# Two PSUM tiles instead of one for a step's first products, in a pool that takes over the projections' banks

## The chip, the cores and the metric

The kernel runs on one core of one Trainium2 chip. The metric is the device time of one execution in microseconds (us), lower is better. TensorE is called PE in the profile (PEld is its weight load), VectorE DVE, ScalarE ACT, GpSimd POOL, and SyncE, which only issues DMAs here, SP.

## The reference

Linear attention by exponential features, and a feed-forward layer with a Mish on what it gives:

```python
def phi(x):                                     # x: batch 8, heads 8, seq 576, head_dim 64
    proj = x @ w_phi                            # 64 -> 128
    proj = proj - np.max(np.abs(proj), axis=-1, keepdims=True)
    return np.concatenate([np.exp(proj), np.exp(-proj)], axis=-1)
q_p, k_p = phi(q), phi(k)
kv = einsum('bhsf,bhsd->bhfd', k_p, v); z = k_p.sum(axis=2)
attn = (q_p @ kv) / (q_p . z + 1e-6)
x = attn as (4608 tokens, 512)
h = x @ w_in                                    # 512 -> 2048
g = h * tanh(log1p(exp(h)))                     # Mish; h above 20 as it is
return g @ w_out                                # 2048 -> 512
```

## The kernel before, in words

All is float32. The program has one list of events, each with a planned time, sorted by that time; what stands in the sorted list is the order of every engine's queue. No engine changes its order at run time, so each stands still until the instruction at its head has what it waits for.

The first stage, to about 292 us, is the attention; its projections (`project`) go to PSUM tiles of two banks, tag `pp` of the pool `ps_a`, which has two of them and so holds four of the eight banks. The pool `ps_b` holds the other four, one bank for each of its tiles. The results go to DRAM (`x_spill`).

The second stage is the feed-forward layer. Tokens come in nine blocks of 512 (`sc`), the 2048 hidden units in eight blocks of 256 (`fp`). A step `n` is one `sc` with one `fp`; there are 72. The steps of one `sc` that follow each other without a break are a segment: four segments of two steps (steps 0 to 7), then sixteen of four. For each segment the activations are loaded (`x_load`), combined (`x_sum`) and split into a high and a low part (`x_block`: ACT casts the high one, DVE subtracts for the low one, seven blocks `xc`). A float32 product is made of three matmuls on such parts.

`h` of a step, 2 x 2 blocks of 128 x 256, comes out of a Winograd form of the 2 x 2 block product, with seven products instead of eight. With `h` as two banks of two halves, the step runs so:

- `ff_in(n, 0)`, PE: products 0 and 1 go to the two halves of the first bank, products 2 and 3 to the two halves of the second; six matmuls each, 24 in all.
- `first_product`, ACT: copies product 0 out as `p1`. `winograd` 0, 1, 2, DVE: `u2` = product 1 + `p1`; `u4` = product 2 + `u2`; the fourth block of `u` = product 3 + `u4`.
- `ff_in(n, 1)`, PE: product 4 is added onto product 0 in the first bank, products 5 and 6 onto 2 and 3 in the second bank; 18 matmuls.
- `mish(n, 0)`, ACT, reads the first bank's half 0; `winograd` 3, DVE, reads the whole second bank and adds `u2`; `mish(n, 1)`, `g_hi` (ACT) and `g_lo` (DVE) make the Mish and its two parts `gh` and `gl`.
- `ff_out`, PE: 24 matmuls of 128 x 512 on `gh`, `gl` and `wout`, in two halves. Products of older steps lie between the two parts of `ff_in`.

In the order written for steady steps PE runs 24 matmuls of `ff_in(n+1, 0)`, 12 of `ff_out`, 18 of `ff_in(n+1, 1)`, 12 of `ff_out`; ACT runs `p1` of step n+1 ahead of `mish(n, 1)` and `g_hi(n)`.

Between DMAs and the 16 pieces of weights that are still to be converted at that time (`weight_ops` with `quiet`: DVE and POOL, lines L124 to L186, in the second stage to about 603 us) the DVE queue also holds `x_sum` (L365), the low parts of `x_block` (L374) and the additions of `drain` (L462).

Waits are put in by the recording layer, by tile: two accesses to one PSUM tile by different engines are ordered by the last access to that tile, whichever of its banks it was. `h` of a step is one tile, `[P, 2, 2, CH]`, that uses the tag `pp` of `ps_a` after the projections:

```python
h_live[n] = ps_a.tile([P, 2, 2, CH], F32, tag="pp", name=f"h_{n}")
```

Of the kernel before, what the change touches and what calls it, by code (L numbers as in the profile page):

```python
# [8 lines left out]
F32 = mybir.dt.float32  # L9
F32R = mybir.dt.float32r  # L10
U32 = mybir.dt.uint32
AF = mybir.ActivationFunctionType
ALU = mybir.AluOpType
AX = mybir.AxisListType
PSUM = bass.MemoryType.PSUM

P = 128
# [5 lines left out]
CH = 256  # L23
# [34 lines left out]
def attention_then_mish(ctx, tc, qT, kT, va, w_phi, w_in, w_out, out):  # L58
    nc = tc.nc

    const = ctx.enter_context(tc.tile_pool(name="const", bufs=1))
    ffn = ctx.enter_context(tc.tile_pool(name="ffn", bufs=2))
    ps_a = ctx.enter_context(tc.tile_pool(name="ps_a", bufs=2, space=PSUM))
    ps_b = ctx.enter_context(tc.tile_pool(name="ps_b", bufs=4, space=PSUM))
    att_scope = ExitStack()
    att = att_scope.enter_context(tc.tile_pool(name="att", bufs=2))
    late = None
# [279 lines left out]
    xT, xc, h_live, u_live, g_live, o_live, part_live = {}, {}, {}, {}, {}, {}, {}  # L347
# [29 lines left out]
    def ff_in(n, which):  # L377
        s, sc, fp, first, last = steps[n]
        assert not any(("in", fp, k) in pieces_left for k in range(2))
        if which == 0:  # L380
            h_live[n] = ps_a.tile([P, 2, 2, CH], F32, tag="pp", name=f"h_{n}")
        for i in range(4) if which == 0 else range(4, 7):
            wb, xb, bank, half = PRODUCTS[i]
            ps = h_live[n][:, bank, half]
            m = 0
            for k in range(2):
                wh, wl = win[fp][:, k, 0, wb], win[fp][:, k, 1, wb]
                xh, xl = xc[s][xb][:, 0, k], xc[s][xb][:, 1, k]
                for w, x in ((wh, xh), (wh, xl), (wl, xh)):
                    nc.tensor.matmul(ps, w, x, start=(i in (0, 2) and m == 0), stop=(m == 5), skip_group_check=True)  # L390
                    m += 1

    def first_product(n):
        p1 = ffn.tile([P, CH], F32, tag="p1", name=f"p1_{n}", bufs=2)
        nc.scalar.copy(p1, h_live[n][:, 0, 0])  # L395
        u_live[n] = [p1]

    def winograd(n, i):
        ps = h_live[n]
        if i == 0:  # L400
            u2 = ffn.tile([P, CH], F32, tag="u2", name=f"u2_{n}", bufs=2)
            nc.vector.tensor_tensor(u2, ps[:, 0, 1], u_live[n][0], op=ALU.add)  # L402
            u_live[n].append(u2)
        if i == 1:
            u4 = ffn.tile([P, CH], F32, tag="u4", name=f"u4_{n}", bufs=1)
            nc.vector.tensor_tensor(u4, ps[:, 1, 0], u_live[n][1], op=ALU.add)
            u_live[n].append(u4)
        if i == 2:
            u = ffn.tile([P, 4, CH], F32, tag="u", name=f"u_{n}", bufs=2)
            nc.vector.tensor_tensor(u[:, 3], ps[:, 1, 1], u_live[n][2], op=ALU.add)  # L410
            u_live[n].append(u)
        if i == 3:
            u2, u = u_live[n][1], u_live[n][3]
            nc.vector.tensor_tensor(u[:, 1:3], ps[:, 1], u2.unsqueeze(1).broadcast_to([P, 2, CH]), op=ALU.add)  # L414

    def mish(n, which):
        u = u_live[n][3]
        if which == 0:
            nc.scalar.activation(u[:, 0], h_live[n][:, 0, 0], AF.Mish)  # L419
        else:  # L420
            nc.scalar.activation(u[:, 1:4], u[:, 1:4], AF.Mish)  # L421
            del h_live[n]
# [58 lines left out]
    def at(time, fn, *args):  # L481
        events.append((time, len(events), fn, args))

    def base(step):
        if step < 0:
            return step * LEAD_STEP
        return min(step, NU - LEAD) * STEP + max(0, step - NU + LEAD) * TAIL_STEP
# [33 lines left out]
    begin = base(NU + 2) + JOIN  # L521
# [5 lines left out]

    at(begin - 0.5, close)

    def t_of(n):  # L530
        return begin + 5.6 + (n - AHEAD) * FFSTEP if n >= AHEAD else begin - PRE[0] + PRE[1] * n

# [16 lines left out]
    for s, (sc, fps) in enumerate(segs):  # L549
        n = steps.index((s, sc, fps[0], True, fps[0] == fps[-1]))  # L550
        t = t_of(n - 2) if n >= AHEAD + 2 else begin - (X0_AT[0], 20)[s]
        at(t + 1.0, x_load, s, sc)
        for i in range(4):
            at(t + 5.5 + 0.7 * i, x_sum, s, i)
        t = t_of(n - 1) if n >= AHEAD + 2 else begin - (X0_AT[1], 3.9)[s]
        for b in range(7):
            at(t + (4.9 if n >= AHEAD + 2 else 3.5) + 0.8 * b, x_block, s, b)
    for n, (s, sc, fp, first, last) in enumerate(steps):
        t = t_of(n)
        at(t, ff_in, n, 0)  # L560
        at(t + 0.75, first_product, n)
        for i in range(3):
            at(t + 1.5 + 0.7 * i, winograd, n, i)
        second = t + 5.7 if n >= AHEAD else t + 3.0
        at(second, ff_in, n, 1)
        at(second + 2.3, winograd, n, 3)
        after = t_of(n + 1) if n >= AHEAD else begin - 2.0 + 2 * n
        at(second + 0.8 if n >= AHEAD else begin - 2.0 + 2 * n, mish, n, 0)
        at(after + 0.9, mish, n, 1)
        at(after + 1.8, g_hi, n)  # L570
        at(after + (3.7 if n >= AHEAD else 2.8), g_lo, n)
        out_a = (begin + 0.9, t_of(n + 1) + 2.8, t_of(n + 1) + 7.8)[min(n, 2)]
        out_b = t_of(n + 2) + 2.85 if n else begin + 2.7
        at(out_a, ff_out, n, 0)
        at(out_b, ff_out, n, 1)
        if last:
            at(t - 4.0 if n >= AHEAD else begin, part_load, s, sc)
            for tt in range(4):
                at((out_a, out_b)[tt // 2] + 1.4 * (tt % 2 + 1) + 0.1, drain, n, tt)
# [3 lines left out]
    for fp in range(HALF, NFP):  # L583
        n = max(i for i, st in enumerate(steps) if st[2] == fp - HALF)
# [41 lines left out]
```

## Time and profile before

| | |
|---|---|
| median of 3 runs | 1071.36 us (1069.99 to 1073.84) |
| the profiled execution's own time | 1071.71 us |
| its span, first to last instruction | 1069.9 us |
| mean granted clock of PE | 0.996 |
| busy: PE, PEld, DVE, ACT, POOL | 98%, 89%, 63%, 47%, 24% of the span |
| first product of the feed-forward layer starts at | 293.2 us |

The profiled execution lies 0.35 us above the median. In rows of the timeline the columns are the start in us, the duration in us of the merged row, engine, line, operation, tiles and count; in brackets stands how long the engine had been idle and whose instruction ended that.

### The profile page before, as it was taken

What the parts mean: (1) busy time and instruction counts of PE and PEld (TensorE: products, weight loads), DVE (VectorE), ACT (ScalarE), POOL (GpSimd) and SP (SyncE); (2) the same over time, 40 slices, a digit from 0 to 9 for tenths busy, and PEclk for the clock granted to TensorE, in tenths of its full rate; (3) what the DMA queues carried; (4) which work ended last, traced back from release to release, by engine and by line L of the source; (5) the groups of instructions that cost most, each with busy time, mean ns of one, the idle gap of its engine ahead of it and who ended that gap; (6) DMA issues with size and microseconds to landing.
All of it is one profiled execution on the core that took longest, in us unless ns stands there. A gap on an engine that the chain in (4) does not pass through costs nothing.

```text
span 1069.9 us, 25646 instructions
## 1 busy us (share of the span) xinstructions
PE 1049.1 (98%) x11200; PEld 951.5 (89%) x11200; DVE 672.7 (63%) x1005; ACT 497.5 (47%) x870; POOL 251.5 (24%) x213
## 2 busy tenths in 40 slices
PE   7999999999989999999999999999999999999998
PEld 7899999998979889998989899999999999999997
DVE  5888888877646877576575653554554546554543
ACT  4777777767744444344443433432332424324321
POOL 0544425532610454345462300000000000000000
PEclk9999999999999999999999999999999999999999
DMA  5545646666437525414424217543032131230221
GB/s 190 184 148 168 207 139 244 223 203 204 169 125 290 192 94 187 158 60 153 168 75 158 74 45 265 207 158 116 14 109 75 44 119 39 81 119 20 99 79 40
DMA packets 62943, 145.53 MB, mean 136 GB/s; under 512 B 5104, under 2 KB 25712, under 8 KB 60016
## 3 DMA queue, kind: packets, MB, share of 16 engines
q1 hardware_dynamic: 62832, 143.90, 38.7%
q8 instruction: 88, 1.44, 0.5%
q14 instruction: 23, 0.19, 0.1%
HBM read 96.17 MB, written 47.71 MB: 134 GB/s over the span
## 4 chain that ended last, share of the span: by engine, by line
PE 92%; DVE 4%; ACT 1%; DMA 1%; issue 1%; POOL 1%; SPq 0%; DVEq 0%; POOLq 0%
PE o L454 34%; PE h L390 32%; PE kvps L225 7%; PE num L225 7%; PE dt L293 4%; PE pp_q L210 4%; PE pp_k L210 4%; DVE xc L374 2%; PE xt L336 2%; DMA x<-x_spill 1%; DVE gl L431 0%; DVE u L414 0%; POOL w_in L168 0%; DMA kraw<-kT 0%; ACT xc L373 0%
## 5 line engine op out<-in xcount | busy, mean ns | idle before, releaser
L390 PEld LDWEIGHTS h<-xc,win 128*128 128x128 f32 x3024 | 381.7, 192 | 19.8 <-issue 5.5
L390 PE MATMUL h<-xc,win 128*128 128x256 f32 x3024 | 387.2, 283 | 6.6 <-DVE u L410 5.4
L454 PE MATMUL o<-wout,gh 128*128 128x512 f32 x1152 | 358.5, 392 | 0.0
L454 PEld LDWEIGHTS o<-wout,gh 128*128 128x128 f32 x1152 | 207.6, 189 | 36.0
L454 PE MATMUL o<-wout,gl 128*128 128x512 f32 x576 | 224.3, 389 | 2.1 <-DVE gl L431 2.1
L402 DVE TENSOR_TENSOR u<-h,p 128x256 f32<-128x256 f32 x72 | 30.5, 424 | 213.6 <-ACT p L395 213.6
L395 ACT COPY p<-h 128x256 f32<-128x256 f32 x72 | 26.8, 372 | 294.0 <-PE h L390 294.0
L454 PEld LDWEIGHTS o<-wout,gl 128*128 128x128 f32 x576 | 108.2, 188 | 26.7 <-DVE gl L431 3.2
L431 DVE TENSOR_TENSOR gl<-u,gh 128x1024 fp32r<-128x1024 f32 x72 | 92.3, 1283 | 31.9 <-ACT gh L426 31.9
L419 ACT ACTIVATE u<-h 128x256 f32<-128x256 f32 x72 | 27.7, 384 | 148.0 <-PE h L390 143.1
L299 ACT ACTIVATE e_q<-dt 128x512 f32<-128x512 f32 x144 | 77.2, 598 | 19.8 <-PE dt L293 19.6
L225 PE MATMUL kvps<-v,e_k 128*64 128x65 f32 x2560 | 83.0, 224 | 2.2 <-issue 1.2
L225 PEld LDWEIGHTS kvps<-v,e_k 128*64 128x64 f32 x2560 | 79.5, 140 | 3.0 <-issue 1.3
L414 DVE TENSOR_TENSOR u<-h,u 128x512 f32<-128x512 f32 x72 | 49.5, 687 | 48.8 <-ACT u L419 47.7
L426 ACT CAST gh<-u 128x1024 fp32r<-128x1024 f32 x72 | 75.8, 1053 | 2.2
L225 PE MATMUL num<-kv,e_q 128*64 128x65 f32 x2304 | 75.0, 223 | 0.0
L225 PEld LDWEIGHTS num<-kv,e_q 128*64 128x64 f32 x2304 | 70.1, 137 | 4.4 <-issue 0.3
L374 DVE TENSOR_TENSOR xc<-x,xc 128x512 fp32r<-128x512 f32 x76 | 57.6, 775 | 8.4 <-ACT xc L373 8.3
L421 ACT ACTIVATE u<-u 128x768 f32<-128x768 f32 x72 | 61.3, 851 | 2.7 <-DVE u L414 2.7
L216 DVE TENSOR_REDUCE m_k<-pp_k 128x8 f32<-128x1024 f32 x36 | 43.9, 1219 | 14.3 <-PE pp_k L210 14.3
L210 PE MATMUL pp_k<-w_phi,kraw 64*128 64x128 f32 x576 | 43.4, 291 | 5.5 <-DMA kraw<-kT 4.0
L216 DVE TENSOR_REDUCE m_q<-pp_q 128x8 f32<-128x1024 f32 x36 | 43.8, 1217 | 6.7 <-PE pp_q L210 6.7
(67 smaller groups left out, 1126.1 us busy)
## 6 DMA issues: line engine op xcount, KB each, us to landing
x<-x_spill SPq DMA_DIRECT2D x40, 512.0 KB, 5.9
o_part<-part SPq DMA_DIRECT2D x11, 1024.0 KB, 4.8
part<-o_part SPq DMA_DIRECT2D x11, 1024.0 KB, 7.6
in_spill<-wst_in SPq DMA_DIRECT2D x12, 896.0 KB, 4.5
win<-in_spill SPq DMA_DIRECT2D x12, 896.0 KB, 6.4
v<-va SPq DMA_DIRECT2D x32, 325.0 KB, 3.3
kraw<-kT SPq DMA_DIRECT2D x36, 256.0 KB, 3.9
qraw<-qT SPq DMA_DIRECT2D x36, 256.0 KB, 4.4
```

The lines of the kernel that those rows point to most:

```text
L210: nc.tensor.matmul(ps[:, j, n], raw[rows, n * P:(n + 1) * P], w_phi2[rows], start=True, stop=True)
L216: nc.vector.tensor_reduce(m, ps, axis=AX.X, op=ALU.max, apply_absolute_value=True)
L225: nc.tensor.matmul(ps[rows], lhsT[:, rows], rhs[h], start=start, stop=stop, skip_group_check=True)
L293: nc.tensor.transpose(ps[:, i * P:(i + 1) * P], e[:, 0, i * P:(i + 1) * P], ident)
L299: nc.scalar.activation(e[:, s, :], ps, AF.Exp, scale=2.0 * s - 1.0)
L374: (nc.vector if s else nc.gpsimd).tensor_tensor(blk[:, 1], src, blk[:, 0].bitcast(F32), op=ALU.subtract)
L390: nc.tensor.matmul(ps, w, x, start=(i in (0, 2) and m == 0), stop=(m == 5), skip_group_check=True)
L414: nc.vector.tensor_tensor(u[:, 1:3], ps[:, 1], u2.unsqueeze(1).broadcast_to([P, 2, CH]), op=ALU.add)
L421: nc.scalar.activation(u[:, 1:4], u[:, 1:4], AF.Mish)
L426: nc.scalar.copy(gh, u_live[n][3])
L431: nc.vector.tensor_tensor(gl, u_live.pop(n)[3], g_live[n][0].bitcast(F32), op=ALU.subtract)
L454: nc.tensor.matmul(ps, g, w, start=(first and f == k == 0), stop=(last and f == 1 and k == 2))
```

## The change

`h` of a step becomes two tiles of one bank each, `h0` and `h1`, in a new pool `ps_h` with two of each. The pool of the projections, `ps_a`, gets a scope of its own and is closed at the planned time `begin - 12.0`, 0.28 ahead of the first `ff_in`; `ps_h` is opened there with waits by tile and has its four banks. `ps_b` is opened ahead of `ps_a`. Products, readers and arithmetic stay as they are.

```diff
-    ps_a = ctx.enter_context(tc.tile_pool(name="ps_a", bufs=2, space=PSUM))
+    proj_scope = ExitStack()
     ps_b = ctx.enter_context(tc.tile_pool(name="ps_b", bufs=4, space=PSUM))
+    ps_a = proj_scope.enter_context(tc.tile_pool(name="ps_a", bufs=2, space=PSUM))
+    ps_h = None
...
-            h_live[n] = ps_a.tile([P, 2, 2, CH], F32, tag="pp", name=f"h_{n}")
+            h_live[n] = [ps_h.tile([P, 2, CH], F32, tag=f"h{i}", name=f"h{i}_{n}") for i in range(2)]
...
-            ps = h_live[n][:, bank, half]
+            ps = h_live[n][bank][:, half]
...
-        nc.scalar.copy(p1, h_live[n][:, 0, 0])
+        nc.scalar.copy(p1, h_live[n][0][:, 0])
...
-            nc.vector.tensor_tensor(u2, ps[:, 0, 1], u_live[n][0], op=ALU.add)
+            nc.vector.tensor_tensor(u2, hx[:, 1], u_live[n][0], op=ALU.add)
...
-            nc.vector.tensor_tensor(u4, ps[:, 1, 0], u_live[n][1], op=ALU.add)
+            nc.vector.tensor_tensor(u4, hy[:, 0], u_live[n][1], op=ALU.add)
...
-            nc.vector.tensor_tensor(u[:, 3], ps[:, 1, 1], u_live[n][2], op=ALU.add)
+            nc.vector.tensor_tensor(u[:, 3], hy[:, 1], u_live[n][2], op=ALU.add)
...
-            nc.vector.tensor_tensor(u[:, 1:3], ps[:, 1], u2.unsqueeze(1).broadcast_to([P, 2, CH]), op=ALU.add)
+            nc.vector.tensor_tensor(u[:, 1:3], hy, u2.unsqueeze(1).broadcast_to([P, 2, CH]), op=ALU.add)
...
-            nc.scalar.activation(u[:, 0], h_live[n][:, 0, 0], AF.Mish)
+            nc.scalar.activation(u[:, 0], h_live[n][0][:, 0], AF.Mish)
...
+    def projected():
+        nonlocal ps_h
+        proj_scope.close()
+        ps_h = ctx.enter_context(tc.tile_pool(name="ps_h", bufs=2, space=PSUM, reuse_waits="tile"))
+
+    at(begin - 12.0, projected)
```

On all five engines the built program has the same instructions in the same order as before. What differs is what they wait for. Line numbers behind the pools move by 2 (L390 becomes L392).

PE's queue at the second products of step 24, before (`xc_8_4` to `xc_8_6` are the activations' blocks for products 4, 5 and 6; in brackets the engines waited for):

```order
L390 MATMUL h_24_7781<-xc_8_4_7767,win_0_624 128x256 [waits DVE_49,Activation_49]
L390 MATMUL h_24_7781<-xc_8_4_7767,win_0_624 128x256 x5
L390 MATMUL h_24_7781<-xc_8_5_7772,win_0_624 128x256 x6
L390 MATMUL h_24_7781<-xc_8_6_7776,win_0_624 128x256 x6
```

And now:

```order
L392 MATMUL h0_24_7809<-xc_8_4_7795,win_0_624 128x256 [waits DVE_49]
L392 MATMUL h0_24_7809<-xc_8_4_7795,win_0_624 128x256 x5
L392 MATMUL h1_24_7810<-xc_8_5_7800,win_0_624 128x256 [waits DVE_49]
L392 MATMUL h1_24_7810<-xc_8_5_7800,win_0_624 128x256 x5
L392 MATMUL h1_24_7810<-xc_8_6_7804,win_0_624 128x256 x6
```

Before, product 4 waits for the DVE instruction on L410 (the last of the three additions) and for ACT's copy; now it waits for DVE's `u2` alone, and the wait for the last addition stands six matmuls later, at product 5.

DVE's queue at the same step, before:

```order
L402 TENSOR_TENSOR u2_24_7811<-h_24_7781,p1_24_7808 128x256 [waits Activation_49]
L406 TENSOR_TENSOR u4_24_7815<-h_24_7781,u2_24_7811 128x256 [waits DVE_49]
L410 TENSOR_TENSOR u_24_7829<-h_24_7781,u4_24_7815 128x256 [waits DVE_49]
L414 TENSOR_TENSOR u_24_7829<-h_24_7781,u2_24_7811 128x512 [waits Activation_49]
```

And now:

```order
L404 TENSOR_TENSOR u2_24_7840<-h0_24_7809,p1_24_7837 128x256 [waits Activation_49]
L408 TENSOR_TENSOR u4_24_7844<-h1_24_7810,u2_24_7840 128x256 [waits DVE_49,PE_49]
L412 TENSOR_TENSOR u_24_7858<-h1_24_7810,u4_24_7844 128x256 [waits DVE_49]
L416 TENSOR_TENSOR u_24_7858<-h1_24_7810,u2_24_7840 128x512 [waits PE_49]
```

`u4` has a wait for PE of its own now, and the last addition (L414, now L416) waits for PE and no longer for ACT's first Mish. On ACT the rows read alike, but the counts that they wait for differ in every step: `p1` waits for the 12th of the 24 first matmuls and no longer for the 24th, and `mish(n, 0)` for the 6th of the 18 second ones and no longer for the 18th. In the whole program PE has 205 instructions that only wait for a semaphore where it had 279, and DVE 199 where it had 127.

More of the change, by code (lines that the diff above doesn't have):

```diff
@@ L394, in first_product @@
         p1 = ffn.tile([P, CH], F32, tag="p1", name=f"p1_{n}", bufs=2)
-        nc.scalar.copy(p1, h_live[n][:, 0, 0])
+        nc.scalar.copy(p1, h_live[n][0][:, 0])
         u_live[n] = [p1]
     def winograd(n, i):
-        ps = h_live[n]
+        hx, hy = h_live[n]
         if i == 0:
             u2 = ffn.tile([P, CH], F32, tag="u2", name=f"u2_{n}", bufs=2)
-            nc.vector.tensor_tensor(u2, ps[:, 0, 1], u_live[n][0], op=ALU.add)
+            nc.vector.tensor_tensor(u2, hx[:, 1], u_live[n][0], op=ALU.add)
             u_live[n].append(u2)
```

## The prediction

> **What bounds the kernel now.** First the page's busy times:
>
> ```profile
> PE 1049.1 (98%) x11200; PEld 951.5 (89%) x11200; DVE 672.7 (63%) x1005; ACT 497.5 (47%) x870; POOL 251.5 (24%) x213
> ```
>
> PE is busy for all but 20.8 of 1069.9 us. The change takes no matmul away, so it can gain at most what PE waits for `h`. Second, the list of PE's waits (line, who ended the wait, us in total, times, longest), of which these concern the feed-forward layer:
>
> ```profile
> PE h L390 <- DVE u L410: 5.4, 5, 1.9
> PE o L454 <- DVE gl L431: 2.1, 1, 2.1
> PE h L390 <- ACT xc L373: 1.2, 1, 1.2
> ```
>
> 8.7 us in seven waits. Third, PE's busy time (third column) in three stretches:
>
> ```profile
> 350.00:392.00 42.00, 39.50 (x238) 34.45 (x237) 36.88 (x54) 19.85 (x33) 22.29 (x18) 1.00 0.51 182
> 535.00:602.00 67.00, 64.80 (x406) 57.93 (x405) 48.01 (x74) 27.74 (x47) 31.10 (x22) 1.00 0.29 100
> 602.00:1050.00 448.00, 448.00 (x2815) 406.30 (x2814) 221.80 (x353) 150.86 (x251) 2.17 (x2) 1.00 0.28 98
> ```
>
> From 602 on PE never stands still; there nothing can be gained. The waits lie in three places: A at 306 to 312 us, B in the first stretch, C in the second, where DVE also converts weights (DVE's busy time, fifth number, is 88% of B and 72% of C, but 50% of the last stretch). Fourth, the timeline of a steady step, to see why it has no wait:
>
> ```profile
> 640.22 0.37 ACT L395 COPY p<-h 128x256 f32<-128x256 f32 x1 [3.17 <-PE h L390]
> 641.54 0.42 DVE L410 TENSOR_TENSOR u<-h,u 128x256 f32<-128x256 f32 x1
> 642.77 2.32 PE L390 MATMUL h<-xc,win 128*128 128x256 f32 x18
> 645.12 0.38 ACT L419 ACTIVATE u<-h 128x256 f32<-128x256 f32 x1 [2.69 <-PE h L390]
> ```
>
> The copy starts when all 24 first matmuls are through, the last addition ends at 641.96, and PE comes to product 4 only at 642.77: 0.8 us to spare. Where DVE is late by more than that, PE stands.
>
> **The change, part by part.** A matmul of this shape follows the last by 0.12 us (18 in 2.32, the last one's own 0.28 taken off). So `p1` may start 12 x 0.12 = 1.44 us earlier, and `mish(n, 0)` also 12 matmuls, 1.44 us. Behind these on ACT stand `mish(n, 1)` and `g_hi`, which move with them. `u4` still waits for the 24th matmul, but no longer for `p1` and `u2` after it, so the last addition can end up to 0.8 us earlier (0.37 + 0.42). PE's wait for it moves by six matmuls, 0.72 us.
>
> Place A is steps 0 and 1, with no older step to cover the chain:
>
> ```profile
> 301.27 3.12 PE L390 MATMUL h<-xc,win 128*128 128x256 f32 x24
> 304.43 0.37 ACT L395 COPY p<-h 128x256 f32<-128x256 f32 x1 [1.96 <-PE h L390]
> 304.82 1.28 ACT L419 ACT_TABLE_LOAD   x1
> 305.75 0.42 DVE L410 TENSOR_TENSOR u<-h,u 128x256 f32<-128x256 f32 x1
> 306.11 0.38 ACT L419 ACTIVATE u<-h 128x256 f32<-128x256 f32 x1
> 306.32 3.24 PE L390 MATMUL h<-xc,win 128*128 128x256 f32 x18 [1.93 <-DVE u L410]
> 307.13 0.61 ACT L373 CAST xc<-x 128x512 fp32r<-128x512 f32 x1
> 307.64 1.05 ACT L426 CAST gh<-u 128x1024 fp32r<-128x1024 f32 x1
> 309.37 1.05 PE L454 MATMUL o<-wout,gh 128*128 128x512 f32 x2
> 309.60 0.39 ACT L419 ACTIVATE u<-h 128x256 f32<-128x256 f32 x1 [0.92 <-PE h L390]
> 309.88 0.61 ACT L373 CAST xc<-xs 128x512 fp32r<-128x512 f32 x1
> 311.23 1.22 DVE L431 TENSOR_TENSOR gl<-u,gh 128x1024 fp32r<-128x1024 f32 x1
> 312.50 0.50 PE L454 MATMUL o<-wout,gl 128*128 128x512 f32 x1 [2.08 <-DVE gl L431]
> ```
>
> The copy moves from 304.43 to 302.99; the table load, the Mish, the cast and `g_hi` stand back to back behind it, so `gh` ends at 308.69 - 1.44 = 307.25. Product 4 needs `u2` (about 303.9) and follows the first products at 304.23 with no wait. Product 5 needs the last addition: `u4` from 304.43, the addition to about 305.3, and 0.15 as from its end at 306.17 to 306.32: 305.45. PE is through at 307.1, waits for `gh` and runs two matmuls from 307.3, then needs `gl`. Step 1's first Mish, which waited for product 6 at 309.60, now follows `g_hi` at 307.14, the cast 0.28 later, and `gl` 1.35 after the cast as in the rows: 308.77, ended at 309.99. PE goes on at 310.04 instead of 312.50: **2.5 us gained**, though about 2.2 us of wait stay. What is late next is `gl`, behind `gh`.
>
> Place B is steps 5 to 8:
>
> ```profile
> 351.74 2.21 DVE L431 TENSOR_TENSOR gl<-u,gh 128x1024 fp32r<-128x1024 f32 x1 [0.46 <-ACT gh L426]
> 363.04 0.42 DVE L410 TENSOR_TENSOR u<-h,u 128x256 f32<-128x256 f32 x1
> 363.61 2.39 PE L390 MATMUL h<-xc,win 128*128 128x256 f32 x18 [0.88 <-DVE u L410]
> 375.54 2.39 PE L390 MATMUL h<-xc,win 128*128 128x256 f32 x18 [1.18 <-ACT xc L373]
> 380.51 3.57 PE L390 MATMUL h<-xc,win 128*128 128x256 f32 x24
> 382.05 1.12 DVE L374 TENSOR_TENSOR xc<-x,xc 128x512 fp32r<-128x512 f32 x1
> 387.19 2.38 PE L390 MATMUL h<-xc,win 128*128 128x256 f32 x18 [0.38 <-DVE u L410]
> ```
>
> (The second wait is put down to a cast, but L410 ended 0.15 ahead of it, as ahead of the others.) The three waits and 0.16 of refill each are 2.9 us, but they don't add up. DVE runs here nearly without a break, and at 382 PE waits for DVE's blocks `xc` (24 matmuls take 3.57 instead of 3.0): there PE can be no further ahead than DVE is. DVE gains where it waited for ACT: 0.46 at 351.74, gone since `gh` comes 1.44 earlier, and some 0.1 of such waits before. I take 0.55 up to 382, and the last wait, 0.38 + 0.16, in full, since DVE is 0.55 early and product 5 gives 0.72 more: **1.1 us**. Bounds: 0.5 with no lead of DVE's, 2.9 with all.
>
> Place C is steps 23 to 28:
>
> ```profile
> 545.53 2.32 DVE L431 TENSOR_TENSOR gl<-u,gh 128x1024 fp32r<-128x1024 f32 x1 [1.18 <-ACT gh L426]
> 556.79 2.39 PE L390 MATMUL h<-xc,win 128*128 128x256 f32 x18 [0.69 <-DVE u L410]
> 588.12 1.23 DVE L431 TENSOR_TENSOR gl<-u,gh 128x1024 fp32r<-128x1024 f32 x1 [0.49 <-ACT gh L426]
> 600.62 2.38 PE L390 MATMUL h<-xc,win 128*128 128x256 f32 x18 [1.51 <-DVE u L410]
> ```
>
> Before each wait DVE works without a break from a `gl` that waited for `gh`. `gh` comes about 1.0 and 1.3 us earlier (in the second case the additions ahead of `gl` on DVE are early too), casts of `xc` no longer stand behind a Mish that waits for product 6, and DVE brings that lead to the additions. With the 0.72 both waits go, 0.69 + 1.51 + 2 x 0.16 = 2.5, and 0.24 of PE's wait for the `gl` that ends at 547.85: **2.8 us**. With no lead, 0.72 each: 1.4.
>
> What is added: DVE's 72 waits for PE. The nearest row is PE's own waiting instruction:
>
> ```profile
> L390 PEldq EVENT_SEMAPHORE  x94: 51/51/51, 298.1 to 1052.3; - x94
> ```
>
> 72 x 0.05 = 3.7 us on DVE's queue, beside 1069.9 - 672.7 = 397 us in which DVE is idle. In a steady step the 0.8 us to spare hides 0.05; without that cover, in the four steps of B, it would cost 4 x 0.05 = 0.2, and in the 12 steps of A, B and C at most 0.6. A wait that is only added can gain nothing. I take 0, since the instruction can wait while the addition ahead of it still runs. PE loses 74 such instructions; they ran ahead in its queue and I count them as nothing.
>
> The clock is the last term. Granted clock (third number from the end) by stretch:
>
> ```profile
> 304.08:307.50 3.42, 1.49 (x13) 1.31 (x12) 1.27 (x3) 3.04 (x5) 0.00 (x0) 1.00 0.89 331
> 307.50:310.91 3.41, 2.92 (x13) 2.20 (x11) 1.58 (x3) 2.24 (x5) 0.00 (x0) 0.50 0.48 200
> 310.91:314.32 3.41, 1.82 (x8) 1.53 (x9) 2.86 (x5) 3.41 (x6) 0.00 (x0) 1.00 0.00 0
> ```
>
> After 1.93 us of idleness within 3.41 us the clock was halved for the next 3.41; after 1.6 (the third row) it was not. The 2.2 us left in A lie above 1.93, and behind them PE has work without a break: half speed for 3.41 us loses 1.7 us, less where the stretches' borders fall into the wait. I take **1.5 lost**; bounds 0 and 1.7. The Trainium skill, page "TensorE: Matmul & The Clock Gate", section "Why this matters for your kernels", asks only that there be no idle gaps over about 3 us between bursts, and by that 2.2 us would cost nothing. The rows here disagree, with a drop after 1.93; by the rule the sum would be 1.5 us better, which is a rival below.
>
> Sum: 2.5 + 1.1 + 2.8 - 1.5 = 4.9 us, against the profiled execution's 1071.7: **1066.8 us**. That execution is 0.35 above the median of the runs shown, which I leave in.
>
> **The rivals.** No drop of the clock behind A, since the border of two stretches cuts the 2.2 us in two, or since what is left is shorter than worked out: 6.4 gained, 1065.3; with all of B, 1063.5. For it: 1.6 us of idleness cost nothing; against it: 1.93 did. By the rule of the Trainium skill above this rival would be the rule, wherever the border lies.
>
> DVE gets no lead, since it is bound by its own work and by DMAs: 2.5 + 0.5 + 1.4 - 1.5 = 2.9, 1068.8. For it: DVE's 88% in B; against it: the waits for `gh` of 0.46, 1.18 and 0.49 right at the heads of its busy stretches.
>
> Slower: ACT and DVE now read one bank while PE writes the other of the same step. If that slowed PE's writes, 12 matmuls in each of 72 steps, 864, would pay. From 5.7 ns each (4.9 us / 864) the gain is gone, from 9.4 ns the kernel is slower by over 0.3%; at 12 ns, 10% of their 0.12 us, it would take 1071.7 - 4.9 + 10.4 = 1077.2. Against it: in the steady step `p1` is read while PE writes the banks of `o`, and the copies show no spread:
>
> ```profile
> L395 ACT COPY p<-h x72: 372/372/376, 296.3 to 1050.5; 128x256 f32<-128x256 f32 x72
> ```
>
> Nothing changes, since other waits hold the same instructions: 1071.7. Against it: the waits in the built program differ at just the instructions that PE stood at.
>
> **How the numbers follow.** Chances: the forecast 0.43 (own range 1065.9 to 1068.2), no drop 0.30, no lead 0.18, nothing 0.06, slower 0.03. What 0.3%, 3.2 us, can't tell from no change ends at 1068.1. Faster by more: nearly all of the first two and a third of the third, 0.78; within: 0.19; slower: 0.03. The range reaches from no drop with all of B, 1063.5, less 0.5 for the scatter of the runs, to no lead with a full drop, 1069.0, and 0.6 for that scatter: 1063.0 to 1069.6.
>
> **What would show it.** Right: `p1` starts 1.4 us ahead of the last first matmul's end in steady steps; PE's waits for the last addition fall from six (5.4 and 1.2 us) to A's 0.5 and scraps; the wait for `gl` in A stays at about 2 us, with half a clock in the 3.4 us behind it; at 382 PE waits for `xc` longer than before. Wrong: waits for the last addition of 0.7 us or more left in C (no lead), full clock behind A (no drop), or matmuls of L392 more than 0.12 us apart in the steady part (slower).

## The result, and the profile after

| | before | after |
|---|---|---|
| median of the runs side by side | 1071.07 us (1069.99 to 1073.84, 5 runs) | 1063.85 us (1063.13 to 1065.90, 5 runs) |
| the profiled execution's own time | 1071.71 us | 1065.52 us |
| its span | 1069.9 us | 1063.4 us |

The kernel became faster: the ratio is 0.9936, 95% interval 0.9916 to 0.9955, some 7 us. The forecast was 1066.8 us with a range of 1063.0 to 1069.6; the time lies inside, near the low end, 2.95 below the forecast.

The page's busy times of the changed kernel, answering the first fence of the prediction:

```profile
PE 1048.2 (99%) x11200; PEld 952.1 (90%) x11200; DVE 667.3 (63%) x1005; ACT 497.7 (47%) x870; POOL 252.4 (24%) x213
```

Its list of PE's waits in the feed-forward layer (total us, times, longest). Of 8.7 us in seven waits 3.1 in four are left, and none for the last addition outside place A:

```profile
PE o L456 <- DVE gl L433: 1.9, 1, 1.9
PE h L392 <- DVE xc L376: 0.7, 1, 0.7
PE h L392 <- DVE u L412: 0.3, 1, 0.3
PE o L456 <- ACT gh L428: 0.2, 1, 0.2
```

PE's busy time by stretch (third column) for B and C. C has no idle time left, B 0.76 us:

```profile
348.00:390.00 42.00, 41.24 (x255) 36.91 (x254) 35.77 (x53) 19.23 (x33) 22.25 (x18) 1.00 0.51 182
533.00:600.00 67.00, 67.00 (x420) 60.62 (x419) 45.99 (x72) 29.02 (x49) 32.12 (x23) 1.00 0.29 98
```

The timeline of a steady step, changed kernel. The copy starts 1.41 us ahead of the end of the 24 first matmuls (644.15); the last addition ends at 645.06, and the second products follow at 646.73: 1.67 us to spare where it was 0.8.

```profile
641.11 3.04 PE L392 MATMUL h<-xc,win 128*128 128x256 f32 x24
642.74 0.37 ACT L397 COPY p<-h 128x256 f32<-128x256 f32 x1 [0.85 <-PE h L392]
644.18 0.42 DVE L408 TENSOR_TENSOR u<-h,u 128x256 f32<-128x256 f32 x1 [0.61 <-PE h L392]
644.64 0.42 DVE L412 TENSOR_TENSOR u<-h,u 128x256 f32<-128x256 f32 x1
646.73 2.31 PE L392 MATMUL h<-xc,win 128*128 128x256 f32 x18
```

To see where the time came from, the same rows are laid side by side: the first products (24 matmuls) of steps 0, 5, 10, 23 and 29. Before:

```profile
293.18 3.11 PE L390 MATMUL h<-xc,win 128*128 128x256 f32 x24
346.43 3.04 PE L390 MATMUL h<-xc,win 128*128 128x256 f32 x24
402.67 3.04 PE L390 MATMUL h<-xc,win 128*128 128x256 f32 x24
539.53 3.04 PE L390 MATMUL h<-xc,win 128*128 128x256 f32 x24
605.59 3.04 PE L390 MATMUL h<-xc,win 128*128 128x256 f32 x24
```

And after:

```profile
292.91 3.12 PE L392 MATMUL h<-xc,win 128*128 128x256 f32 x24
345.25 3.04 PE L392 MATMUL h<-xc,win 128*128 128x256 f32 x24
399.15 3.04 PE L392 MATMUL h<-xc,win 128*128 128x256 f32 x24
535.91 3.04 PE L392 MATMUL h<-xc,win 128*128 128x256 f32 x24
599.03 3.04 PE L392 MATMUL h<-xc,win 128*128 128x256 f32 x24
```

The lead of after over before is 0.27, 1.18, 3.52, 3.62 and 6.56 us. The first, 0.27, is scatter of the attention, whose code is the same (over all profiled executions here step 0 started between 290.6 and 293.2). So A (step 0 to 5) gave 0.91, B (5 to 10) 2.34, C (23 to 29) 2.94, and what lies between 0.10. After step 29 nothing changes; the spans differ by 6.56 too. The forecast for A, with its clock drop, was 1.0, for B 1.1, for C 2.8. Only B is off.

### The profile page after: what moved, and what is told of

Read it like the earlier page. It is cut to its first block, busy times and chain, and to the rows that moved or that the text cites. A ratio compares the mean times of both kernels' runs of the same rounds, so it can differ in the third digit from the quotient of the medians.

```text
span 1063.4 us, 25644 instructions
## 1 busy us (share of the span) xinstructions
PE 1048.2 (99%) x11200; PEld 952.1 (90%) x11200; DVE 667.3 (63%) x1005; ACT 497.7 (47%) x870; POOL 252.4 (24%) x213
## 4 chain that ended last, share of the span: by engine, by line
PE 95%; DVE 2%; DMA 1%; ACT 1%; POOL 1%; issue 0%; SPq 0%; DVEq 0%; POOLq 0%
PE o L456 36%; PE h L392 32%; PE kvps L227 7%; PE num L227 7%; PE dt L295 4%; PE pp_q L212 4%; PE pp_k L212 4%; PE xt L338 2%; DVE xc L376 1%; DMA x<-x_spill 1%; DMA kraw<-kT 0%; POOL w_in L170 0%; ACT xc L375 0%; DVE xs L367 0%; POOL t_in L151 0%
## 5 line engine op out<-in xcount | busy, mean ns | idle before, releaser
L392 PEld LDWEIGHTS h<-xc,win 128*128 128x128 f32 x3024 | 381.5, 191 | 12.5 <-DVE xc L376 1.2
L392 PE MATMUL h<-xc,win 128*128 128x256 f32 x3024 | 386.0, 283 | 1.0 <-DVE xc L376 0.7
L416 DVE TENSOR_TENSOR u<-h,u 128x512 f32<-128x512 f32 x72 | 49.5, 688 | 78.5 <-PE h L392 78.4
L408 DVE TENSOR_TENSOR u<-h,u 128x256 f32<-128x256 f32 x72 | 30.6, 425 | 37.7 <-PE h L392 37.1
```

The lines of the kernel that those rows point to most:

```text
L416: nc.vector.tensor_tensor(u[:, 1:3], hy, u2.unsqueeze(1).broadcast_to([P, 2, CH]), op=ALU.add)
```

## The experiments

For each kernel A, B and C are the growth of the lead over before between the same steps, from the starts of the same rows. The last column is the lead with which the activations loaded for step 8 reach DVE (in the kernel before at 368.24, shown below), less the kernel's own lead at step 5; it is used for B. Differences of 0.01 to the text come from rounding.

| kernel | median us, ratio [interval] | A | B | C | lead of the load |
|---|---|---|---|---|---|
| after | 1063.85, 0.9936 [0.9916, 0.9955] | 0.90 | 2.35 | 2.93 | 1.79 |
| pool alone | 1071.42, 0.9996 [0.9980, 1.0012] | -1.94 | 1.27 | 0.01 | 1.26 |
| first bank last | 1065.59, 0.9949 [0.9934, 0.9963] | 0.22 | 1.27 | 2.57 | 1.26 |
| copy late, new tile | 1064.78, 0.9945 [0.9928, 0.9962] | -0.64 | 2.40 | 1.67 | 1.90 |
| copy late, in place | 1069.64, 0.9987 [0.9975, 0.9999] | -1.89 | 2.50 | 1.08 | 1.94 |
| `gl` first | 1062.28, 0.9918 [0.9899, 0.9936] | 3.91 | 2.61 | 2.93 | 2.06 |
| resume later | 1064.24, 0.9942 [0.9924, 0.9960] | 0.87 | 3.65 | 2.93 | 5.80 |
| 64 bytes | 1060.28, 0.9898 [0.9882, 0.9914] | 2.32 | 2.29 | 3.24 | 1.79 |
| `gl` first and 64 bytes | 1059.07, 0.9893 [0.9876, 0.9909] | 3.73 | 2.32 | 3.24 | 1.83 |
| last blocks of x later | 1063.71, 0.9931 [0.9911, 0.9951] | 0.93 | 2.87 | 2.93 | 2.31 |
| last blocks of x earlier | 1063.71, 0.9933 [0.9915, 0.9951] | 1.13 | 2.30 | 2.93 | 1.73 |
| before with 64 bytes | 1067.87, 0.9976 [0.9964, 0.9987] | -0.26 | 0.61 | 0.31 | 0.67 |

**The pool alone.** The own pool and its early opening stay, but `h` is one tile of two banks in it, so the waits are those of before.

```diff
-            h_live[n] = [ps_h.tile([P, 2, CH], F32, tag=f"h{i}", name=f"h{i}_{n}") for i in range(2)]
+            ht = ps_h.tile([P, 2, 2, CH], F32, tag="h", name=f"h_{n}")
+            h_live[n] = [ht[:, 0], ht[:, 1]]
```

> The new pool and the banks it takes over stay, but a step's h is one tile of two banks again. Theory (what counts is that waits go by bank): all waits are back, PE's wait for the last addition in five or six places, 6.6 us, time within 0.2% of before, 1071. Rival (the pool's own scope or its place in PSUM brings part of it): faster than before by 1 us or more.

PE's waits of this kernel:

```profile
PE h L393 <- DVE u L413: 4.5, 4, 1.9
PE o L457 <- DVE gl L434: 2.1, 1, 2.1
PE h L393 <- ACT xc L375: 1.0, 1, 1.0
```

The waits are back and the time is that of before. What works is the two tiles. This execution came out of A 1.94 us later, with two stretches of half clock instead of one, and B gave 1.27 of it back; C gave 0.01.

**First bank last.** Products 5 and 6, on the second bank, run ahead of product 4. The copy of product 0 is still early, but `mish(n, 0)` has to wait for all 18 second matmuls again, and PE needs the last addition first, without the cover of six matmuls.

```diff
-... (2, 4, 0, 0), (6, 5, 1, 0), (1, 6, 1, 1))
+... (6, 5, 1, 0), (1, 6, 1, 1), (2, 4, 0, 0))
```

> Two tiles as in the changed kernel, but the second products run in the order 5, 6, 4: PE meets the last addition at the first of the 18 matmuls (the cover of six matmuls is gone), and the first Mish waits for the 18th. The early copy stays. Theory (the early copy gives ACT and DVE the lead): place C's first wait stays away, of its second 0.2 to 0.4 us come back, A loses about 0.75, B some 0.5; 1.3 to 1.7 us slower than the changed kernel, span about 1065. Rival (the six matmuls are what counts): both waits of C back with 0.7 and 1.5 us, span 1067.5 or more.

```profile
PE o L456 <- DVE gl L433: 2.4, 1, 2.4
PE h L392 <- DVE u L412: 2.3, 3, 1.0
```

1.7 us slower than the changed kernel by the medians. A loses 0.7, B 1.1, C only 0.4 (0.75, some 0.5 and 0.2 to 0.4 were expected): in C the early copy carries most.

**Copy late, two forms.** A copy of one column from the second bank stands ahead of `p1` on ACT, so `p1` waits for the 24th matmul as before; the early Mish and the cover of six matmuls stay. In the first form the column goes to a tile of its own:

```diff
+        z = ffn.tile([P, 1], F32, tag="z", name=f"z_{n}", bufs=2)
+        nc.scalar.copy(z, h_live[n][1][:, 1, 0:1])
         nc.scalar.copy(p1, h_live[n][0][:, 0])
```

> Two tiles as in the changed kernel, but ahead of each step's copy ACT copies one column of the second bank, so the copy waits for the 24th matmul as before and comes some 0.2 us later still. The six matmuls of cover and the early Mish stay. Theory (the early copy counts): each wait for the last addition comes back less about 0.5 us (0.4 and 1.2 left in C), A gains 0.5 instead of 2.5; about 2 us faster than before, span about 1067.8. Rival (the six matmuls and the early Mish count): span about 1064.5, no more than 1.5 us slower than the changed kernel.

This run could not be read as meant: the steady step, in which nothing should change, became shorter, 10.479 us instead of 10.520 (mean of steps 40 to 69), and the lead grew by 2 us from step 29 to 71. The new tile takes 64 bytes and moves the tiles behind it. The second form writes the column into `p1` itself, and no tile moves:

```diff
+        nc.scalar.copy(p1[:, 0:1], h_live[n][1][:, 1, 0:1])
         nc.scalar.copy(p1, h_live[n][0][:, 0])
```

> As the last but one (copy held back to the 24th matmul, cover of six matmuls and early Mish kept), but the small copy goes to a column of p1 itself, so no tile in SBUF moves; in the run before, matmuls of the steady part were spaced otherwise (step 10.48 instead of 10.52 us), which hid what the copy is worth. Theory (the early copy carries A and half of C, cover and early Mish carry B): against the changed kernel A loses 1.5, B 0.2, C 1.2; span about 1066 from the same start of the first product, steady step 10.52. Rival (early copy counts for little): span within 1 us of the changed kernel's.

```profile
PE h L392 <- DVE u L405: 1.8, 2, 1.1
```

By the medians 5.8 us of the gain are gone, by the leads 4.5: 2.8 in A, where the chain copy, `u2`, Mish, `gh`, `gl` is bare and the clock was halved for 6.83 us, and 1.9 in C (1.5 and 1.2 were expected). PE now waits at product 4 for `u2` (L405, the row). With the early copy alone C gave 2.57, with the early Mish and the cover alone 1.08, with both 2.93, with neither 0.01. B hardly cares: 2.50. (The added copy itself holds ACT for 0.16 us a step.)

**`gl` first.** `g_lo` of step 0 goes two places ahead on DVE, so that the wait that stays in A goes too.

```diff
-        at(after + (3.7 if n >= AHEAD else 2.8), g_lo, n)
+        at(after + (3.7 if n >= AHEAD else 2.8 if n else 2.05), g_lo, n)
```

> The changed kernel with step 0's low part of the Mish two places further ahead on DVE, so that PE's wait of 1.9 us in A falls to 0.3 to 0.6 and the clock should not drop behind it. Forecast as on record (terms add, the drop costs 1.5): 1.4 + 1.5 = 2.9 us faster than the changed kernel, span 1060.5. Rival (in B DVE is the bound, and what PE gains or loses in A is taken back there; DVE itself comes about 1.2 us later here, since step 1's last addition moves behind): PE's wait for the blocks xc near 379 us grows from 1.2 to 4 us or more, span 0 to 1.2 us above the changed kernel's 1063.4.

The wait for `gl` fell from 1.92 to 0.5 us, no stretch of half clock follows A, and A gave 3.91: 3.0 more than in the changed kernel, 1.4 of wait and 1.6 of clock. B and C kept their gains, so what A gives is not taken back.

**Resume later.** The conversion of the weights that are left starts 42.4 us later, out of B.

```diff
-RESUME = 40.03
+RESUME = 82.43
```

> The changed kernel with the second half of the weight conversion starting 42.4 us later, one segment of four steps, so that DVE and POOL have no conversion in B; C's pattern moves by one segment. Theory (B's waits come from DVE's own work): the wait for the blocks xc near 379 us (0.7, 1.2 us by starts) goes, lead over before at step 9 rises from 3.5 to about 4.2; span 0.5 to 1 us below the changed kernel's. Rival (the blocks xc are late for their loads or for ACT): the wait stays.

B gave 3.65, with no wait of PE in it. The conversions now meet the loads at 420, where PE waits (the timeline's row of this kernel) and 0.96 us of lead is lost up to step 20:

```profile
419.67 1.91 PE L392 MATMUL h<-xc,win 128*128 128x256 f32 x11 [0.48 <-DVE xc L376]
```

The time is that of the changed kernel, where 0.5 to 1 us less was expected. What bounds B is the conversions, with their DMAs, together with the loads of activations; putting them elsewhere moves the place.

**64 bytes.** To find out what the first form of the late copy had done, its tile is kept for steps 0 and 1 only, where it is filled from the first bank and holds nothing up; the shift in SBUF stays for all steps.

```diff
+        if n < 2:
+            z = ffn.tile([P, 1], F32, tag="z", name=f"z_{n}", bufs=2)
+            nc.scalar.copy(z, h_live[n][0][:, 0, 0:1])
```

> The changed kernel with a tile of one column, in two buffers of 32 bytes, put between p1 and u2 in SBUF and written by ACT in steps 0 and 1 alone: u, gh, gl, the last two xc buffers and win and wout 2 and 3 move by 64 bytes, nothing else changes. If the place in SBUF set the matmuls' spacing in the run with the late copy: steady step 10.48, 2 to 3 us faster than the changed kernel. If the 72 added copies did it: step 10.52, within 0.5 us of the changed kernel.

> Step 0's low part of the Mish further ahead on DVE, and the shift by 64 bytes. If both add: no drop of the clock behind A, steady step 10.48, 4 us faster than the changed kernel, 1060. If the shift does nothing: as without it, 1062.3.

The second kernel joins this to `gl` first. The groups of PE from 640 to 1040 us (count, busy us, mean ns of one), changed kernel:

```profile
L392 PE MATMUL h<-xc,win 128*128 128x256 f32 x1596 | 203.4, 283 | 0.0
L456 PE MATMUL o<-wout,gl 128*128 128x512 f32 x305 | 118.6, 389 | 0.0
```

And with the 64 bytes:

```profile
L392 PE MATMUL h<-xc,win 128*128 128x256 f32 x1597 | 199.6, 280 | 0.0
L459 PE MATMUL o<-wout,gl 128*128 128x512 f32 x307 | 121.0, 394 | 0.0
```

Per step 42 matmuls of the first kind become shorter and 8 of the second longer, and the 16 on `gh` go from 392 to 393 ns; the step becomes 0.04 us shorter, near 3 us in all. A gave 1.4 us more than in the changed kernel, since no half clock followed it in this execution. By the medians the 64 bytes give 3.6 us. Joined with `gl` first the time is 1059.07 us, the lowest here, though its interval overlaps that of 64 bytes alone.

**Before with 64 bytes.** The same tile in the kernel before.

> The kernel before with the same 64 bytes in steps 0 and 1 (a tile of one column that ACT writes), which move the tiles behind them in SBUF. If the shorter step (10.48 us where it was 10.52) comes from the place in SBUF alone, the steady steps take 10.48 here too, and the time is 2.5 to 3.5 us below the kernel before, about 1067.7; the waits for h stay (8 to 9 us in all). If it takes the two tiles for h, the steady step stays at 10.52 and the time at 1070.7, a little above for the added copies.

```profile
PE h L390 <- DVE u L413: 4.9, 5, 2.0
```

1067.87 us against 1070.34 side by side: 2.5 us less, with PE's waits for the last addition still there (the row). The steady step is 10.479 us here too. So the shorter step comes without the two tiles too: it is not the change's.

**Last blocks of x later, and earlier.** The timelines show what stood behind B. Before, POOL's last subtraction on a piece of weights, DVE's last two blocks that read the loaded activations, SP's load of the next, and DVE's first instruction on it:

```profile
357.92 2.68 POOL L177 TENSOR_TENSOR wst_in<-w_in,wst_in 128x896 fp32r<-128x896 f32 x1 [1.05 <-ACT wst_in L173]
357.94 3.22 DVE L374 TENSOR_TENSOR xc<-x,xc 128x512 fp32r<-128x512 f32 x2
361.18 1.94 SPq L353 DMA_DIRECT2D x<-x_spill  x2
368.24 0.69 DVE L365 TENSOR_TENSOR xs<-x 128x512 f32<-128x512 f32 x1 [3.31 <-DMA x<-x_spill]
```

The same after, and PE at the block that comes of it:

```profile
354.71 2.67 POOL L179 TENSOR_TENSOR wst_in<-w_in,wst_in 128x896 fp32r<-128x896 f32 x1 [1.06 <-ACT wst_in L175]
354.72 3.20 DVE L376 TENSOR_TENSOR xc<-x,xc 128x512 fp32r<-128x512 f32 x2
357.95 1.94 SPq L355 DMA_DIRECT2D x<-x_spill  x2
365.28 0.69 DVE L367 TENSOR_TENSOR xs<-x 128x512 f32<-128x512 f32 x1 [3.96 <-DMA x<-x_spill]
379.23 1.91 PE L392 MATMUL h<-xc,win 128*128 128x256 f32 x11 [0.68 <-DVE xc L376]
```

The activations have one buffer (tile `x32`). The load leaves 0.02 to 0.03 us after DVE's last reading and lands 7 us later; DVE stands for the last 3.3 to 4.0 us of that, and the block that PE waits for starts on DVE 13.8 us after that in both kernels, at 382.05 before and at 379.10 after. The theory made of it: B is a loop through that buffer. The two kernels move the last reading by one instruction, for the load of step 8 alone.

```diff
+            place = 3.5 if (s, b) == (3, 6) else b
-            at(t + (4.9 if n >= AHEAD + 2 else 3.5) + 0.8 * b, x_block, s, b)
+            at(t + (4.9 if n >= AHEAD + 2 else 3.5) + 0.8 * place, x_block, s, b)
```

> In steps 5 and 6 the low part of block 6 (made from the sums) goes ahead of the addition and of blocks 4 and 5 (made from the loaded activations), on DVE and ACT; nothing else moves. Theory 1 (the size of B is set by a loop through the single buffer of loaded activations: DVE's last block that reads it releases the next load, which lands 7 us later, and DVE then works without a break to the block that PE waits for): the load at 358 us is issued 0.6 to 1.1 us later, lands as much later, PE's wait for xc at 379 grows from 0.7 to 1.3 to 1.8, and B gives 1.2 to 1.7 us where the changed kernel had 2.3; all other gains stay; the time is 0.6 to 1.1 above the changed kernel's, 1064.5 to 1065. Theory 2 (the prediction's: DVE is bound by its own work and only gains where it waited for ACT): the work is the same, B stays at 2.3 and the wait at 0.7.

In the other, `place` is 3.4 and 3.5 for blocks 4 and 5 of that segment, and `b` for all others.

> At the same place blocks 4 and 5 go ahead of the last addition of step 5 on DVE, so that the buffer of loaded activations comes free one instruction (0.60 us) earlier; on ACT the cast of block 5 goes ahead of a weight cast. Theory 1 (the loop through that buffer): the load is issued and lands 0.5 to 0.7 us earlier than in the changed kernel, PE's wait for xc at 379 falls from 0.7 to at most 0.2, B gives 2.8 to 3.0. Theory 2 (DVE's own work): B stays at 2.3. A third way: the addition, 3 us later, makes the Mish and gl of step 5 late, and PE waits for gl near 363.

Load, landing and PE's wait, later reading:

```profile
354.82 3.03 DVE L376 TENSOR_TENSOR xc<-x,xc 128x512 fp32r<-128x512 f32 x2
357.88 1.50 SPq L355 DMA_DIRECT2D x<-x_spill  x2
364.24 0.69 DVE L367 TENSOR_TENSOR xs<-x 128x512 f32<-128x512 f32 x1 [3.56 <-DMA x<-x_spill]
378.19 1.91 PE L392 MATMUL h<-xc,win 128*128 128x256 f32 x11 [0.19 <-DVE xc L376]
```

And earlier reading, where SP's store of weights stands ahead of the load:

```profile
351.72 2.15 DVE L376 TENSOR_TENSOR xc<-x,xc 128x512 fp32r<-128x512 f32 x3
355.88 0.32 SPq L195 DMA_DIRECT2D in_spill<-wst_in  x1
356.30 1.96 SPq L355 DMA_DIRECT2D x<-x_spill  x2
363.79 0.69 DVE L367 TENSOR_TENSOR xs<-x 128x512 f32<-128x512 f32 x1 [4.13 <-DMA x<-x_spill]
377.74 1.91 PE L392 MATMUL h<-xc,win 128*128 128x256 f32 x11 [0.70 <-DVE xc L376]
```

Both expectations of theory 1 failed at the load, and its other half held. Issued 0.44 us later (against the kernel's own lead at step 5), the load landed 0.52 earlier, since it took 6.36 us instead of 7.33; and B gave 0.52 more, with the wait down to 0.19. In the other kernel the buffer was free at 353.87, but the load stood in SP's queue behind the store of `in_spill`, which waited for POOL's subtraction to end at 355.85, until 356.30, only 0.11 earlier than in the changed kernel, and took 7.49 us; it landed 0.06 later, and B gave 2.30. The forecast of theory 2, that B stays as it is because DVE's work does, failed in the first kernel, and the rows speak against it: in all four timelines DVE stands 3.3 to 4.1 us for the load. The 0.52 itself is the difference of two single executions; by the medians both kernels take 1063.71 us, against 1063.85 of the changed kernel, which tells nothing apart.

The last column of the table carries this through all kernels but one: where the last wait of B is gone, B is the lead of the load plus 0.49 to 0.57 (eight kernels); where it is kept (pool alone, first bank last, before with 64 bytes), the lead of the load plus -0.06 to 0.01. The exception is the kernel without the conversions, where the load is 5.80 early and PE has no wait left to lose. So in these executions B goes with when the load lands.

The landing itself goes with the conversion of a piece of weights. SP's store of that piece (`in_spill`) stands ahead of the load in SP's queue and leaves when POOL's last subtraction ends. DVE can use the load 7.5 to 7.9 us after the store, whether the load left 0.4 or 1.2 us behind it. That holds in all twelve kernels with a conversion here; in the one without, the load took 5.57 us from its start. This is read from the rows; no run moved the store alone. In the table "words" is the time from SP's load of that piece of weights, still unconverted (`words_in`), to POOL's first use of it, and "use" is DVE's first instruction on the loaded activations.

| kernel | words | POOL ends | store leaves | load leaves | use | use after store |
|---|---|---|---|---|---|---|
| before | 7.12 | 360.60 | 360.63 | 361.18 | 368.24 | 7.61 |
| after | 6.55 | 357.38 | 357.41 | 357.95 | 365.28 | 7.87 |
| pool alone | 6.11 | 361.35 | 361.38 | 361.93 | 368.98 | 7.60 |
| last blocks of x later | 6.36 | 356.70 | 356.72 | 357.88 | 364.24 | 7.52 |
| last blocks of x earlier | 6.03 | 355.85 | 355.88 | 356.30 | 363.79 | 7.91 |
| before with 64 bytes | 6.50 | 359.15 | 359.18 | 359.72 | 366.72 | 7.54 |

DVE's last reading hangs on the same subtraction: it takes 2.62 us before and 2.60 after, where such a block takes 0.67 to 0.70 us wherever POOL is idle. Of the changed kernel's lead of 1.79, 0.98 was there when SP issued the load of `words_in`, since the load of activations ahead of it, for step 6, had waited for DVE's last reading too; 0.57 is the shorter time of that load, 0.50 came between that and POOL's end, and 0.26 was lost behind it. Of the 1.26 of pool alone 1.00 is the shorter time of that load. So B moves with the time of a transfer, without any change of waits: the three kernels with the waits of before (before, before with 64 bytes, pool alone) gave 0, 0.61 and 1.27. Why this load took 6.0 to 7.3 us was not tried.

## Why the prediction was right, and where it was wrong

- A, 2.5 us: right. Changed kernel, timeline:

```profile
305.11 1.69 PE L392 MATMUL h<-xc,win 128*128 128x256 f32 x12 [0.26 <-DVE u L412]
308.42 1.22 DVE L433 TENSOR_TENSOR gl<-u,gh 128x1024 fp32r<-128x1024 f32 x1
309.69 0.50 PE L456 MATMUL o<-wout,gl 128*128 128x512 f32 x1 [1.92 <-DVE gl L433]
```

PE goes on at 309.69, with the 0.27 of scatter taken off 2.54 us earlier than before; `gl` was forecast for 308.77 and came at 308.42, 308.69 on the scale of before, and the wait for it is 1.92 where 2.2 was said.

- The clock, 1.5 lost: right in this execution, 1.63 (2.54 at 309.69, 0.91 at step 2 and step 5). The stretches of 3.41 us, granted clock third from the end, changed kernel:

```profile
307.40:310.81 3.41, 1.49 (x7) 0.94 (x6) 2.85 (x5) 3.41 (x6) 0.00 (x0) 1.00 0.51 207
310.81:314.22 3.41, 3.41 (x10) 2.64 (x9) 3.35 (x5) 1.24 (x3) 0.00 (x0) 0.50 0.00 0
```

The rival without a drop is as real: 64 bytes has the same wait, 1.93 us, but a border of two stretches cuts it differently and PE is busy for 1.60 us of this one:

```profile
305.60:309.02 3.42, 1.60 (x7) 1.33 (x8) 3.13 (x5) 3.42 (x6) 0.00 (x0) 1.00 0.18 74
309.02:312.43 3.41, 3.41 (x17) 2.71 (x16) 2.86 (x4) 0.76 (x2) 0.00 (x0) 1.00 0.00 0
```

Five kernels had this wait of 1.92 to 1.93 and this order of work; four had the drop. Where the stretches lie differs from execution to execution, so the term is a chance of some 1.6 us, and the forecast treated it rightly as one. By the Trainium skill, page "TensorE: Matmul & The Clock Gate", section "What's actually happening", the window of 3413 ns runs free of the kernel; the traces agree (two drops of one execution, pool alone, lay two windows of 3.41 us apart, at 307.23 and 314.05). Its section "Why this matters for your kernels", weighed in the prediction, warns of gaps over about 3 us only; the rows disagree, 1.92 us of idleness were enough.

- B, 1.1 us: this step failed. "I take 0.55 up to 382" was the term: it counted only DVE's waits for ACT as what DVE could gain, since "DVE runs here nearly without a break". The load's landing, 2.96 us earlier by the rows above and 1.79 without the lead that PE brought from A, moved DVE's whole stretch up to the block at 379, and the wait of 3.31 us for that load stood in DVE's timeline before. The other term, the last wait's 0.54 in full, was right: 0.56. How much of the 1.24 above the forecast is the change's own stays open: 0.57 of the lead is the shorter time of the load of `words_in`, and kernels with the waits of before differ by 1.27 in B. The upper bound of 2.9 held the 2.34; it left out what PE loses at 380, where 24 matmuls take 3.57 us instead of 3.04.
- C, 2.8: right, 2.94, with both waits gone and 0.26 of the wait for `gl`. That DVE would bring its lead to the additions shows in the wait of `gl` for `gh`, 1.18 before:

```profile
540.47 2.31 DVE L433 TENSOR_TENSOR gl<-u,gh 128x1024 fp32r<-128x1024 f32 x1 [0.60 <-ACT gh L428]
```

- DVE's added waits, 0: right. `u4` waits 0.61 us for PE in a steady step, and 1.67 us are to spare; the steady step is 10.520 us before and after.
- Slower through the banks: refuted. The matmuls of L392 take 283 ns in the steady part, as those of L390 did, and 24 still take 3.04 us. Nothing changes: refuted with the result; pool alone shows what it would have looked like.
- The sum: 2.54 - 1.63 + 2.34 + 2.94, 0.10 elsewhere and 0.27 of scatter are 6.56, the difference of the spans, against 4.9 forecast. 1.2 of the 1.7 is B. That the medians lie 7.2 apart and the profiled executions 6.2 is within the scatter of a single execution (the five runs of after spread over 2.8 us). Of the 2.95 us by which the median lies below the forecast, 1.28 is what the profiled execution lies below it; the other 1.67 is that execution's distance to the median, which no trace explains.

## What to carry to other kernels

A wait is worth no more than the distance to what is late next, and that can be a transfer: where an engine's busy stretch begins with a wait for a load, follow the load back to its buffer's last reader, its queue and its transfer time before the stretch is called bound by its own work. One profile of each kernel is little for that: B differed by 1.27 us between kernels with the same waits. Two halves of one change are not worth their sum or their parts everywhere: the early copy carried A and C, and B came out the same without it. A shift of some bytes in SBUF can be worth a third to a half of such a change, so an experiment that adds a tile needs a partner that adds only the tile.

## What was not expected of the hardware

The 64 bytes: a tile of one column ahead of the others changed the mean duration of the matmuls of 128x256 from 283 to 280 ns and of those on `gl` from 389 to 394, the step from 10.520 to 10.479 us and the time by 2.5 to 3.6 us, with the change and without. Which of the moved operands does it was not tried.

The clock: of the stretches at full clock in A in which PE was idle, ten with PE busy for 0.95 to 1.55 of 3.41 us were followed by half a clock, those with 1.71 and 1.82 were not, and of two between, 1.60 and 1.66, only the second was. So the limit lies between 1.55 and 1.71 us of PE's busy time as the records show it, and it is not sharper. A stretch already at half clock is another case: with PE busy for 2.60 us another half followed (copy late, in place), with 2.92 and more none did.

DVE beside POOL: a block `xc` on DVE took 0.67 to 0.70 us in the second stage wherever POOL was idle (102 of the 126 from 320 us on, before) and up to 2.62 us beside one of POOL's subtractions.
